# Loading residual rows earlier, two sums on another engine, and a reordered turn in a two-layer attention and MLP kernel

## The chip, the cores and the metric

The kernel runs on one core of one Trainium2 chip. The metric is the time of one execution on the device, in microseconds (us), as a median over several runs.

Five engines matter. TensorE (PE in the profile) multiplies matrices, VectorE (DVE) and ScalarE (ACT) work on elements, GpSimd (POOL) issues part of the transfers, and the DMA engines move data. Each engine executes its own queue; semaphores make one wait for another.

## The reference, cut to what matters

Two layers, each an attention part A and a token-mixing MLP part B, with residual additions, on x of 2048 rows by 1024 columns in bf16:

```python
# A: h = layernorm(x); q, k, v = h @ wqkv, 32 heads of 32
W, dil = 8, 2                      # each row attends to 8 rows: itself and every second one before it
idx = pos[:, None] - (jnp.arange(W) * dil)[None, :]
logits = einsum("bhsd,bhswd->bhsw", q, k[idx]) * scale      # masked where idx < 0
o = einsum("bhsw,bhswd->bhsd", softmax(logits), v[idx])
x = x + o @ wo
# B: h = layernorm(x); mixes over the 2048 rows, F = 3584
x = x + (gelu(h.T @ w1 + b1) @ w2 + b2).T
# ... and both once more
```

Rows of even and of odd position never attend to each other. The kernel calls them the two classes (c = 0 and 1), 1024 rows each, eight tiles of 128 rows.

## The kernel before

For each class the attention runs over two blocks of heads of four head groups each; with two classes there are four blocks, n = 0 to 3. For a block VectorE multiplies queries by shifted keys (`T`, 2.28 us each), TensorE sums these products per head (`sc`), a softmax follows on VectorE and ScalarE, and the probabilities `Pb` go out to memory (`pd`) and come back spread over the partitions (`pb`). VectorE multiplies them by the values (`pr`) and adds the eight products of each row; the sums (`oT`) feed the output projection. All work is written as generators that are woven together, and the order within each engine's queue is then settled by a scheduler when the kernel is built.

```python
def softmax_back(self, n):
    nc.vector.tensor_tensor(out=m4[:], in0=L[:, 0:4, :], in1=L[:, 4:8, :], op=ALU.add)
    ...                                            # two more sums, a reciprocal
    nc.vector.tensor_tensor(out=Pb[:], in0=L[:], in1=..., op=ALU.mult)
    nc.gpsimd.dma_start(out=dst, in_=Pb[:]...)     # pd <- Pb
    self.spread(n)                                 # two loads pb <- pd, 1 MB each

def pv(self, n, dq):                               # block n, head group dq
    for hf in range(2):                            # two halves of the rows
        pr = tpl.tile([P, 4, W, TB], BF16, name="pr", tag="T")
        ...                                        # two products pr <- pb, v
        if (n, dq) in self.pe_pv:                  # sum on TensorE: eight identity matmuls into PSUM
            for s in range(W):
                nc.tensor.matmul(acc[:]..., lhsT=ident[:], rhs=pr[:, :, s, :], start=(s == 0), stop=(s == W - 1))
            nc.scalar.copy(out=oT[:, hf * HT:(hf + 1) * HT], in_=acc[:])
        else:                                      # sum on VectorE in three steps
            for wd in (4, 2):
                nc.vector.tensor_tensor(out=pr[:, :, 0:wd, :], ..., op=ALU.add)
            nc.vector.tensor_tensor(out=dst, in0=pr[:, :, 0, :], in1=pr[:, :, 1, :], op=ALU.add)
```

The output projection of one class takes eight row tiles; for class 0 the residual rows `xr` are added by an identity matmul on TensorE. The loop loads each tile's rows at its start, from GpSimd:

```python
for i in range(NT):
    xr = x2("xr")                                  # x2: a pool with four slots
    nc.gpsimd.dma_start(out=xr[:], in_=res[i])
    ...
    for n in range(NDC):
        for kt in range(KD):
            nc.tensor.matmul(ps[:], lhsT=at_.oT[c][kt][:, i * P:(i + 1) * P], rhs=wo_t[n][kt // 4][:, kt % 4, :], ...)
        nc.tensor.matmul(ps[:], lhsT=ident[:], rhs=xr[:, xs_], start=False, stop=True)
```

Two more places are touched. At the start, eight transposed tiles `hT` are copied out of PSUM, half of them by VectorE and half by ScalarE. At the turn from layer 0 to layer 1, the last tiles of class 1 pass a layernorm (`hb`) on ScalarE, a transpose on TensorE and a copy to `hT`, and the first keys and queries of class 1 follow.

## Time and profile before

| | before |
|---|---|
| median of the first 3 runs | 1375.02 us (1372.79 to 1375.53) |
| span of the profiled run | 1371.8 us |
| TensorE busy | 1290.6 us, 94% |
| TensorE idle | 81.2 us |
| VectorE busy | 664.7 us, 48% |
| ScalarE busy | 494.0 us, 36% |

The profile also cuts the span into 40 slices of 34.3 us. A digit is the busy share of a slice in tenths, and PEclk is the clock that TensorE was granted, in tenths. TensorE's and its clock's rows for the kernel before:

```profile
PE   5899996999999999999997989979999999999997
...
PEclk9999998999999999999999999999999999999999
```

Between the opening and the last slice there are few digits under 9: the seventh (206 to 240 us, layer 0's first output projection; its clock falls too), and the 22nd, 24th and 27th, of which the 27th (892 to 926 us) is the same place in layer 1.

### The profile page before, as it was taken

What the parts mean: (1) busy time and instruction counts of PE and PEld (TensorE: products, weight loads), DVE (VectorE), ACT (ScalarE), POOL (GpSimd) and SP (SyncE); (2) the same over time, 40 slices, a digit from 0 to 9 for tenths busy, and PEclk for the clock granted to TensorE, in tenths of its full rate; (3) what the DMA queues carried; (4) which work ended last, traced back from release to release, by engine and by line L of the source; (5) the groups of instructions that cost most, each with busy time, mean ns of one, the idle gap of its engine ahead of it and who ended that gap; (6) DMA issues with size and microseconds to landing.
All of it is one profiled execution on the core that took longest, in us unless ns stands there. A gap on an engine that the chain in (4) does not pass through costs nothing.

```text
span 1371.8 us, 15564 instructions
## 1 busy us (share of the span) xinstructions
PE 1290.6 (94%) x6306; PEld 584.9 (43%) x6432; DVE 664.7 (48%) x782; ACT 494.0 (36%) x860; POOL 95.9 (7%) x231
## 2 busy tenths in 40 slices
PE   5899996999999999999997989979999999999997
PEld 3444332444444444444443434434444444444443
DVE  5366999879602332225774117976783034111111
ACT  6945443853222430123534455548322234000000
POOL 3000000100100000000001000001010000000000
PEclk9999998999999999999999999999999999999999
DMA  9134344382623235552758631335635232334341
GB/s 246 46 92 124 97 111 122 104 211 72 191 62 92 73 118 170 176 169 65 190 150 201 185 123 62 102 82 162 153 108 153 62 92 70 113 100 139 99 122 49
DMA packets 213753, 166.71 MB, mean 122 GB/s; under 512 B 6833, under 2 KB 201393, under 8 KB 211633
## 3 DMA queue, kind: packets, MB, share of 16 engines
q1 hardware_dynamic: 198656, 110.11, 28.5%
q0 software_dynamic: 14448, 54.55, 13.8%
q8 instruction: 50, 0.82, 0.3%
q10 hardware_dynamic: 576, 1.05, 0.2%
q14 instruction: 23, 0.18, 0.0%
HBM read 146.81 MB, written 18.87 MB: 121 GB/s over the span
## 4 chain that ended last, share of the span: by engine, by line
PE 67%; issue 7%; ACT 6%; DVE 3%; DMA 3%; POOL 0%; POOLq 0%; ACTq 0%
PE ps L580 27%; PE ps L602 23%; PE ps L375 10%; PE ps L547 5%; DMA w<-in_B_w_dram 1%; DMA xr<-xb 1%; PE sc L402 1%; ACT xn L551 1%; DMA xr<-in_A_x_dram 1%; DVE xo L607 1%; ACT h L229 1%; ACT h L218 1%; PE tp L234 1%; DVE pr L455 1%; DVE pr L467 1%
## 5 line engine op out<-in xcount | busy, mean ns | idle before, releaser
L602 PE MATMUL ps<-g,w 128*128 128x512 bf16 x1750 | 389.8, 380 | 8.8 <-DMA w<-in_B_w_dram 6.3
L580 PE MATMUL ps<-h,w 128*128 128x512 bf16 x1754 | 386.1, 379 | 4.1 <-ACT h L229 2.2
L375 PE MATMUL ps<-hT,wq 128*128 128x512 bf16 x1128 | 261.4, 385 | 10.3 <-ACT hT L302 4.2
L602 PEld LDWEIGHTS <-w 128*128 128x128 bf16 x1792 | 174.5, 98 | 218.9 <-DMA w<-in_B_w_dram 7.3
L580 PEld LDWEIGHTS <-w 128*128 128x128 bf16 x1792 | 175.3, 98 | 214.3 <-issue 3.3
L397 DVE TENSOR_TENSOR T<-q,k 128x4096 bf16<-128x4096 bf16 x64 | 144.0, 2288 | 107.5 <-ACT q L377 62.4
L607 DVE SCALAR_TENSOR_TENSOR xo<-ps,b_sb,xs 128x512 bf16<-128x512 f32 x64 | 48.0, 750 | 301.8 <-PE ps L602 285.7
L375 PEld LDWEIGHTS <-wq 128*128 128x128 bf16 x1152 | 114.2, 101 | 149.8 <-issue 26.0
L591 DVE TENSOR_TENSOR tmp<-ps,g 128x512 f32<-128x512 f32 x80 | 55.3, 692 | 202.3 <-PE ps L580 198.2
L467 DVE TENSOR_TENSOR pr<-pr 128x2048 bf16<-128x2048 bf16 (+1 forms) x128 | 120.5, 949 | 0.3
L547 PE MATMUL ps<-wo,oT 128*128 128x512 bf16 x376 | 95.7, 386 | 8.5 <-DVE oT L469 8.0
L455 DVE TENSOR_TENSOR pr<-pb,g 128x2048 bf16<-128x2048 bf16 x64 | 77.3, 1220 | 31.9 <-DMA pb<-pd 19.3
L592 ACT ACTIVATE g<-tmp,b_sb 128x512 bf16<-128x512 f32 x80 | 57.7, 721 | 82.1 <-DVE tmp L591 82.1
L375 PE MATMUL ps<-hT,wv 128*128 128x512 bf16 x372 | 86.1, 380 | 0.9 <-issue 0.4
L380 ACT CAST k<-ps 128x1024 bf16<-128x1024 f32 x64 | 64.6, 1014 | 46.0 <-PE ps L375 32.3
L455 DVE TENSOR_TENSOR pr<-pb,v 128x2048 bf16<-128x2048 bf16 x64 | 76.4, 1217 | 5.5 <-DMA pb<-pd 5.5
L586 ACT CAST g<-ps 128x512 bf16<-128x512 f32 x80 | 46.2, 586 | 76.0 <-PE ps L580 73.5
L547 PEld LDWEIGHTS <-oT 128*128 128x128 bf16 x384 | 37.4, 99 | 66.1 <-issue 15.1
L191 ACT ACTIVATE ln<-mv,eps 128x1 f32<-128x1 f32 x34 | 10.0, 293 | 141.8 <-DVE mv L200 137.5
L375 PEld LDWEIGHTS <-wv 128*128 128x128 bf16 x384 | 42.3, 114 | 41.8 <-issue 5.5
L377 ACT CAST q<-ps 128x512 bf16<-128x512 f32 x64 | 37.4, 588 | 53.1 <-PE ps L375 51.9
L588 ACT ACTIVATE g<-ps,b_sb 128x512 bf16<-128x512 f32 x32 | 22.0, 687 | 83.2 <-PE ps L580 83.2
(97 smaller groups left out, 703.9 us busy)
## 6 DMA issues: line engine op xcount, KB each, us to landing
w<-in_B_w_dram SPq DMA_DIRECT2D x96, 448.0 KB, 4.7
w<-in_B_w_dram SPq DMA_DIRECT2D x56, 512.0 KB, 4.8
wq<-in_A_wqkv_dram SPq DMA_DIRECT2D x40, 512.0 KB, 3.8
pb<-pd POOLq DMA_DIRECT2D x16, 1024.0 KB, 11.4
wo<-in_A_wo_dram SPq DMA_DIRECT2D x16, 512.0 KB, 3.8
xa<-xn POOLq DMA_DIRECT2D x32, 256.0 KB, 2.4
xs<-xa POOLq DMA_DIRECT2D x32, 256.0 KB, 4.3
wv<-in_A_wqkv_dram SPq DMA_DIRECT2D x12, 512.0 KB, 9.4
```

Source lines behind the costliest of these rows:

```text
L375: nc.tensor.matmul(ps[:], lhsT=cols, rhs=self.hT[c][hf][:, kt, :], start=(kt == 0), stop=(kt == KD - 1))
L380: nc.scalar.copy(out=window(buf, 0, PADK + hf * HT, [(KW + 1, 2), (1, HT)]), in_=ps[:].unsqueeze(1).to_broadcast([P, 2, HT]))
L397: nc.vector.tensor_tensor(out=T[:], in0=q[:].unsqueeze(1).to_broadcast([P, 4, SC]), in1=window(k, par, 2, [(2, 4), (1, SC)]), op=ALU.mult)
L455: nc.vector.tensor_tensor(out=pr[:, :, u, :], in0=pb[:, :, u, :], in1=window(v, par, 2 + hf * HT, [(TB, 4), (2, 4), (1, TB)]), op=ALU.mult)
L467: nc.vector.tensor_tensor(out=pr[:, :, 0:wd, :], in0=pr[:, :, 0:wd, :], in1=pr[:, :, wd:2 * wd, :], op=ALU.add)
L547: nc.tensor.matmul(ps[:], lhsT=at_.oT[c][kt][:, i * P:(i + 1) * P], rhs=wo_t[n][kt // 4][:, kt % 4, :], start=(kt == 0), stop=(kt == KD - ...
L580: nc.tensor.matmul(ps[:], lhsT=wt[c][:, i, fl * P:(fl + 1) * P], rhs=h2[c][i // 4][:, i % 4, dc * 512:(dc + 1) * 512], start=(k == 0), sto ...
L586: nc.scalar.copy(out=gs, in_=ps[:])
L591: nc.vector.tensor_tensor(out=tmp[:], in0=ps[:], in1=gs, op=ALU.add)
L592: nc.scalar.activation(out=gs, in_=tmp[:], func=ACT.Gelu_apprx_tanh, bias=b1_sb[:, ft:ft + 1])
L602: nc.tensor.matmul(ps[:], lhsT=w2t[ft // HF][:, ft % HF, c::DIL], rhs=g[ft // GF][:, ft % GF, dc * 512:(dc + 1) * 512], start=(ft == 0), s ...
L607: nc.vector.scalar_tensor_tensor(out=xo[:, dc * 512:(dc + 1) * 512], in0=ps[:], scalar=b2_sb[:, i, c:c + 1], in1=xs[:, dc * 512:(dc + 1) * ...
```

## The change

Four things at once: the residual rows are fetched two tiles ahead; two of the sums of layer 0 (head groups 2 and 3 of the second block) move from VectorE to TensorE, so that the output projection doesn't wait for VectorE; one hT copy goes from ScalarE to VectorE; and at the turn the first keys and queries of class 1 are made per half of the rows, with the last two layernorms on VectorE.

```diff
-            copy = nc.vector.tensor_copy if i % 4 in (1, 2) else nc.scalar.copy
+            copy = nc.scalar.copy if i in (0, 3, 4) else nc.vector.tensor_copy
@@ proj_pair
+            if c and pair == 0 and 0 in parts:
+                for hf in range(2):
+                    for part in parts:
+                        for dt in range(2):
+                            yield self.proj(c, part, dt, hf)
+                return
             for part in parts:
                 for hf in range(2):
@@ out_proj
+        xrs = []
+
+        def fetch():
+            if len(xrs) < NT:
+                xrs.append(x2("xr"))
+                nc.gpsimd.dma_start(out=xrs[-1][:], in_=res[len(xrs) - 1])
+
+        fetch()
+        fetch()
         for i in range(NT):
-            xr = x2("xr")
-            nc.gpsimd.dma_start(out=xr[:], in_=res[i])
+            xr = xrs[i]
...
+            fetch()
             nc.gpsimd.dma_start(out=dst_v[i], in_=xn[:])
@@ for li in range(2)
-        at_ = Attn(li, hT, ())
+        at_ = Attn(li, hT, {(1, 2), (1, 3)} if first else ())
...
-                    yield from gemm2_tile(1, i, w2_tiles(i), xa[0], xb[1][i * P:(i + 1) * P, :], hT, on_act=True)
+                    yield from gemm2_tile(1, i, w2_tiles(i), xa[0], xb[1][i * P:(i + 1) * P, :], hT, on_act=i < NT - 2)
```

## The prediction

> **What bounds the kernel now.** I read the busy table first, then TensorE's waits, then the stretches around the longest of them instruction by instruction.
>
> ```profile
> PE 1290.6 (94%) x6306; PEld 584.9 (43%) x6432; DVE 664.7 (48%) x782; ACT 494.0 (36%) x860; POOL 95.9 (7%) x231
> ```
>
> TensorE is busy for 1290.6 of 1371.8 us. From 309 us to 652 us and from 995 us to the end it hardly waits, so nothing in those stretches can give much back. What the change can win is some part of TensorE's 81 us of idle time, and what it adds to TensorE costs its full length wherever TensorE had work. The list of TensorE's waits says where the idle time is (columns: total, times, longest):
>
> ```profile
> PE ps L550 <- DMA xr<-xb: 8.6, 2, 8.3
> PE ps L547 <- DVE oT L469: 8.0, 1, 8.0
> ...
> PE ps L550 <- DMA xr<-in_A_x_dram: 5.6, 2, 5.0
> PE tp L234 <- ACT hb L229: 5.0, 6, 2.7
> PE ps L375 <- ACT hT L302: 4.2, 2, 3.1
> ```
>
> Five single waits matter, and each has a part of the change aimed at it: 8.3 and 5.0 (residual rows), 8.0 (a PV sum on VectorE), 2.7 (the last layernorm of the second class, ScalarE) and 3.1 (an hT copy). The residual wait of layer 1, in TensorE's timeline:
>
> ```profile
> 893.11 0.62 PE L402 MATMUL sc<-T,sel 128*32 128x512 bf16 x8
> 902.05 0.58 PE L550 MATMUL ps<-xr,ident 128*128 128x512 bf16 x1 [8.33 <-DMA xr<-xb]
> 902.43 3.00 PE L547 MATMUL ps<-wo,oT 128*128 128x512 bf16 x7
> ```
>
> and GpSimd's, which issues these loads in order:
>
> ```profile
> 886.29 1.05 POOL L440 DMA_DIRECT2D pb<-pd  x2 [3.90 <-DMA pd<-Pb]
> 887.31 0.61 POOL L540 DMA_DIRECT2D xr<-xb  x1
> ```
>
> The row tile that TensorE wants at 893.7 is issued at 887.3, just behind two 1 MB loads of probabilities, and lands at 902.05, 14.7 us later; the usual time to landing of this load is 3.1 us. Layer 0 has the same picture: issued at 226.9 behind the pair at 225.3, wanted at 233.2, landed at 238.2. The first tile's rows (issued at 35.9 and 793.6) wait for nothing.
>
> The wait for a PV sum:
>
> ```profile
> 212.74 1.89 PE L375 MATMUL ps<-hT,wq 128*128 128x512 bf16 x8
> 222.65 0.61 PE L547 MATMUL ps<-wo,oT 128*128 128x512 bf16 x1 [8.02 <-DVE oT L469]
> ```
>
> VectorE is busy for 96.6 of the 98 us from 139 to 237 us; the sum TensorE waits for is the third of the four halves that the change moves (pair groups 2 and 3 of the second head block), ended at 222.6.
>
> There is a second price after a long wait: the seven L547 from 902.43 take 3.00 us, 0.43 us each, against 0.216 us in steady running (eight L547 in 1.73 us). In 902.0 to 905.5 us nine 512-column matmuls take 3.5 us instead of 1.9, with a granted clock of 0.56. By the same count I get about 1.6 us of slow matmuls after the wait at 238.2 (clock 0.50), 1.6 after 222.65 (0.51) and 1.4 after the 3.13 us wait at 33.93 (0.54 to 0.69). The waits of 2.2 and 2.7 us at 195.9 and 806.9 have no such tail.
>
> **What the Trainium skill says.** "TensorE: Matmul & The Clock Gate", Part 1 (the HAM clock gate): after about one 3.4 us window of idleness the array falls to half clock and needs about as long a busy window to recover. The trace agrees: tails of 3 to 4 us at 0.43 us a matmul after waits of 5 to 8 us, none after 2.7 us. "DMA: Bandwidth & Descriptors", SWDGE vs HWDGE vs iDMA: DMAs issued from GpSimd go through rings of which only one queue is allocated, drained packet by packet; so the rows stand behind the probabilities. The trace agrees: 14.7 us against 3.1. "VectorE: DVE Perf Modes", the perf-mode tier table: a bf16 SBUF tensor_tensor runs at 2x at most, 1224 ns for 2048 elements; the trace has 1215 ns for that form of the sums, so they can't be made cheaper on VectorE and moving them is the only saving.
>
> **The change part by part.** All counts are as of TensorE, since the path is TensorE's work plus its waits.
>
> *Rows two tiles ahead.* The number of loads stays. The tile 1 load moves to directly behind tile 0's, hence to about 36 to 50 us and 794 to 802 us, far ahead of the probabilities; what now follows the probabilities is tile 2, wanted only at about 240 and 912 us and landed at about 233 and 902. The x2 pool has four slots; tile i+2 can take a slot when tile i has used its rows, which is the depth of before, so no new wait need arise. Removed: layer 1 8.33 + 0.29 + 1.6 of slow clock = 10.2 us; layer 0 5.0 + 0.58 + 1.6 = 7.2 us. VectorE waits on these same stalls (6.33 us until 906.2 and 5.4 us until 242.4, both for score matmuls stuck behind TensorE's), so it moves forward along with TensorE and the output projection of class 1, at 336 and 1008 us, doesn't turn into a wait. That matters: there VectorE finishes its last sum at 337.5 and 1009.0, level with TensorE. I take 90%: 15.7 us.
>
> *Two PV sums on TensorE.* Two head groups, two halves each: four times (1.215 + 0.684 + 0.42) = 2.32 us leave VectorE, 9.3 us. In come 4 x 8 identity matmuls at 0.216 us = 6.9 us on TensorE and four ScalarE copies of 0.58 us on an engine that is a third busy there. For the third half, VectorE is now two removed halves earlier (4.6 us): its product ends near 212.8, and sum and copy end near 216. TensorE reaches the output projection at 214.6 plus three sums (5.2 us), 219.8, so the 8.0 us wait and its 1.6 us tail go. Net 9.6 - 6.9 = 2.7 us; I take 2.5.
>
> *The eighth hT copy to VectorE.* Now on ScalarE, at 32.9 behind junk and v work; VectorE does its copy of the seventh tile at 30.35 in 0.64 us and could do this one by 31.7. TensorE's 3.13 us wait becomes about 0.9, without the tail: 3.6 us on the spot. But ScalarE is busy nearly without a gap from 30 to 70 us, and TensorE waits for its hT copies at 48 to 54 us (3.0 us in all); ScalarE gains only the 1.0 us copy and an earlier k. I let 1.5 us through.
>
> *Keys by half, and the last two layernorms on VectorE.* At the turn of layer 1 TensorE runs two projection units (16 matmuls, 3.6 us), waits 2.72 for the layernorm, transposes, then waits 1.10 for the hT copy:
>
> ```profile
> 800.53 3.62 PE L375 MATMUL ps<-hT,wq 128*128 128x512 bf16 x16
> 806.86 0.62 PE L234 MATMUL tp<-ident,hb 128*128 128x128 bf16 x8 [2.72 <-ACT hb L229]
> 808.58 10.52 PE L375 MATMUL ps<-hT,wq 128*128 128x512 bf16 x47 [1.10 <-ACT hT L239]
> ```
>
> The new order has four units that need only the first half, 7 us. On VectorE the layernorm is two statistics of 0.69, one of 0.21, ln and exp of 0.5 and the 0.55 scale, some 3 us with handovers, where ScalarE takes about 6.5; in class 0, where it is already on VectorE, TensorE's waits for it are 0.3 us at most. VectorE is idle there. Gain 2.72 + 1.10 + 0.42 (tile 6) = 4.2, of which I take 3.8. In layer 0 the order changes nothing: T needs the seventh unit either way.
>
> Sum: 15.7 + 2.5 + 1.5 + 3.8 = 23.5 us, to 1351.5.
>
> **Rivals.**
> 1. *Another engine takes the place of the wait.* In the first output projection ScalarE needs about 5.2 us a tile and TensorE 3.9; VectorE is full up to 237 us. For it: several end times lie level. Against it: each of these engines is itself held up by the waits that go. If half of the rows' gain and the sums' gain were taken back: about 1361.
> 2. *The rows are late anyway.* If the new load takes its place behind the probabilities all the same, or its slot comes free late because layernorm tiles hold the pool, only the other parts act: about 1367. Against it: the first tile's load was issued 190 us and 90 us early in the same pool.
> 3. *The sums are a loss.* If TensorE had other work to put in the 8 us gap, or the sums stall in order behind VectorE's products, they cost their 6.9 us: about 1358.
> 4. *More than the sum.* VectorE ends layer 0's class 0 some 9 us earlier, which could also remove the small score waits (0.2 to 2.2 us) and let everything through in full: about 1346.
>
> **Range and chances.** The measured waits and tails give an upper sum near 27 to 30 us (the 2% line is 27.5 us, 1347.5); instruction order is set anew by the scheduler at build time, which costs a few us more often than it gives. I predict 1352.0, 1345 to 1362. Faster by over 2% needs nearly every term in full: 0.22. Slower by 2% would need a new stall larger than all seen here: 0.01.
>
> **What would show it.** In the changed profile: no wait of L550 on xr above 1 us and no slow matmuls behind it (layer 1 should lose about 10 us between 880 and 950 us of the old clock); no wait of L547 for a PV sum at the start of the output projection, with 32 new identity matmuls and 12 fewer tensor_tensor on VectorE; the wait at the turn of layer 1 under 1 us; the wait at 33.9 us near 1 us with those for hT just after it grown. It is wrong if the row loads still follow the probabilities, if TensorE's idle time near 340 or 1010 us grows above 2 us, or if its total idle time falls by less than 20 us.

## More of the kernel before

A word on line numbers: the change adds lines, so one instruction has different numbers in different kernels. Before and after, in this order: the product T is L397 and L403, its score matmul L402 and L408, the probabilities L422 and L428, the products with the values L455 and L461, the output projection L547 and L561, its row addition L550 and L564. Experiments shift them by one at times.

## The result, and the profile after

| | median | runs | ratio to before |
|---|---|---|---|
| before | 1375.28 us (1372.79 to 1381.48) | 4 | |
| after | 1361.76 us (1356.69 to 1361.86) | 4 | 0.9886 [0.9846, 0.9926] |
| after, run again with the experiments | 1357.72 us (1356.27 to 1363.10) | 6 | 0.9870 [0.9849, 0.9891] |

A ratio is the mean time of one kernel's runs over the mean of the other's runs in the same rounds, so it isn't quite the ratio of the medians beside it. The change is faster by 1.1 to 1.3%. The time of the first comparison lies at the upper edge of the predicted range. The profiled span fell from 1371.8 to 1360.1 us.

The busy table of the kernel after:

```profile
PE 1296.8 (95%) x6338; PEld 587.5 (43%) x6464; DVE 661.2 (49%) x779; ACT 486.2 (36%) x843; POOL 96.3 (7%) x231
```

TensorE has 32 matmuls more and is busy for 6.2 us longer, its idle time is 1360.1 - 1296.8 = 63.3 us. It fell by 17.9 us, where the prediction asked for at least 20. The same two rows of slices, after:

```profile
PE   5899999799999999999998899999999999999996
...
PEclk9999999899999999999999899999999999999999
```

The digits below 9 at the 24th and 27th slice are gone. The one of the seventh slice has moved to the eighth (238 to 272 us), and the low clock with it. The second low clock, in the 23rd slice, stands behind a wait of 4.01 us for MLP weights at 750.35 us, which no part of the change aims at. So the two layers must be looked at apart. I do that with marks in TensorE's timeline, in us:

| mark | before | after |
|---|---|---|
| layer 0, first MLP matmul | 274.41 | 275.82 |
| layer 1, first projection | 598.83 | 599.68 |
| layer 1, first output projection | 884.64 | 881.83 |
| layer 1, first MLP matmul | 945.87 | 932.75 |
| last matmul's end | 1362.0 | 1350.3 |

From layer 1's first projection to the end it was 763.2 us and is 750.6 now: 12.6 us gained, more than the whole span shows. Layer 0 gained nothing. Layer 1's place of the old 8.33 us wait, TensorE's timeline after (start, duration, engine, line, operation):

```profile
892.59 0.38 PE L564 MATMUL ps<-xr,ident 128*128 128x512 bf16 x1
892.90 0.61 PE L408 MATMUL sc<-T,sel 128*32 128x512 bf16 x8
893.45 13.99 PE L375 MATMUL ps<-hT,wq 128*128 128x512 bf16 x62
```

There is no wait for rows here or anywhere else in the trace, and 62 matmuls follow in 13.99 us, 0.226 us each, so no slow tail either. From the output projection's start to the MLP's start it was 61.2 us and is 50.9: 10.3 us, against 10.2 predicted. The turn:

```profile
803.80 0.62 PE L234 MATMUL tp<-ident,hb 128*128 128x128 bf16 x8
804.25 12.03 PE L375 MATMUL ps<-hT,wq 128*128 128x512 bf16 x54
```

Neither the transpose nor the projection behind it waits any more.

Layer 0 is another matter. TensorE's waits for T in its list of waits, before and then after (total, times, longest):

```profile
PE sc L402 <- DVE T L397: 3.8, 5, 2.2
```

```profile
PE sc L408 <- DVE T L403: 11.3, 7, 5.0
```

The waits for rows and for the PV sum are gone, but waits for T, 3.8 us in all before, are 11.3 us now. The two longest in TensorE's timeline:

```profile
261.50 1.04 PE L408 MATMUL sc<-T,sel 128*32 128x512 bf16 x8 [5.02 <-DVE T L403]
264.88 1.05 PE L408 MATMUL sc<-T,sel 128*32 128x512 bf16 x8 [2.34 <-DVE T L403]
265.86 2.99 PE L561 MATMUL ps<-wo,oT 128*128 128x512 bf16 x8
```

The eight matmuls behind them take 2.99 us, 1.1 us more than the usual 1.89: a slow tail as well. Why does VectorE deliver T so late? VectorE's timeline before, around the probabilities of the third block (n = 2):

```profile
217.37 0.95 DVE L421 RECIPROCAL m<-m 128x128 f32<-128x128 f32 x1
218.23 1.16 DVE L467 TENSOR_TENSOR pr<-pr 128x2048 bf16<-128x2048 bf16 x1
219.31 1.21 DVE L422 TENSOR_TENSOR Pb<-L,m 128x1024 bf16<-128x1024 f32 x1
```

And after:

```profile
216.45 2.28 DVE L403 TENSOR_TENSOR T<-q,k 128x4096 bf16<-128x4096 bf16 x1
218.65 0.41 DVE L425 TENSOR_TENSOR m<-m 128x256 f32<-128x256 f32 x1
218.99 2.28 DVE L403 TENSOR_TENSOR T<-q,k 128x4096 bf16<-128x4096 bf16 x1
221.19 0.28 DVE L426 TENSOR_TENSOR m<-m 128x128 f32<-128x128 f32 x1
221.39 2.28 DVE L403 TENSOR_TENSOR T<-q,k 128x4096 bf16<-128x4096 bf16 x1
223.59 0.94 DVE L427 RECIPROCAL m<-m 128x128 f32<-128x128 f32 x1
224.45 2.22 DVE L403 TENSOR_TENSOR T<-q,k 128x4096 bf16<-128x4096 bf16 x1
226.60 1.21 DVE L428 TENSOR_TENSOR Pb<-L,m 128x1024 bf16<-128x1024 f32 x1
240.75 2.36 DVE L461 TENSOR_TENSOR pr<-pb,g 128x2048 bf16<-128x2048 bf16 x2 [12.94 <-DMA pb<-pd]
```

The steps of the softmax depend on one another, and the scheduler puts other work between them. Before, that was pieces of the sums and a product with the values, of 0.4 to 1.2 us. Now the sums are on TensorE, the product comes earlier, and in their place stand four products T of 2.28 us, each ahead of a step that the probabilities need. Pb starts at 226.60 instead of 219.31. GpSimd's timeline shows what follows, after:

```profile
228.10 0.64 POOL L431 DMA_DIRECT2D pd<-Pb  x1
233.39 1.05 POOL L446 DMA_DIRECT2D pb<-pd  x2 [4.65 <-DMA pd<-Pb]
```

Before, these two stood at 220.81 and 225.30. VectorE, which had work until 237 us in the kernel before, now runs out of it at 227.8 and waits 12.94 us for pb. The products with the values, and behind them the next T, come later, and TensorE waits for that T. The Trainium skill, "TensorE: Matmul & The Clock Gate", section "Architectural detail: the array is 16× 32×32, not 1× 128×128", calls VectorE's queue strictly first in, first out. The trace fits: ScalarE had cast the queries of the next T by 241.56 us, but that T stood behind the products and sums and ran at 259.16.

### The profile page after: what moved, and what is told of

It reads as the page before. It is cut to its first block, busy times and chain, and to the rows that moved or that the text cites.

```text
span 1360.1 us, 15621 instructions
## 1 busy us (share of the span) xinstructions
PE 1296.8 (95%) x6338; PEld 587.5 (43%) x6464; DVE 661.2 (49%) x779; ACT 486.2 (36%) x843; POOL 96.3 (7%) x231
## 4 chain that ended last, share of the span: by engine, by line
PE 74%; DVE 9%; ACT 6%; DMA 6%; issue 4%; POOL 1%; POOLq 0%; DVEq 0%; ACTq 0%
PE ps L595 27%; PE ps L617 23%; PE ps L375 15%; PE ps L561 5%; DVE pr L461 3%; DMA w<-in_B_w_dram 2%; DVE pr L473 2%; PE sc L408 2%; DMA pb<-pd 2%; DVE T L403 1%; DVE xo L622 1%; PE tp L234 1%; DMA b_bf<-in_B_b_dram 1%; DMA pd<-Pb 1%; DVE bn L198 1%
## 5 line engine op out<-in xcount | busy, mean ns | idle before, releaser
L473 DVE TENSOR_TENSOR pr<-pr 128x2048 bf16<-128x2048 bf16 x120 | 112.5, 944 | 0.3
```

The source lines that it names most:

```text
L473: nc.vector.tensor_tensor(out=pr[:, :, 0:wd, :], in0=pr[:, :, 0:wd, :], in1=pr[:, :, wd:2 * wd, :], op=ALU.add)
```

## The experiments

The theory after this reading: in layer 0 the four T products ahead of the probabilities take back what the other parts give. Rivals: the sums just cost TensorE their 6.9 us wherever VectorE's products stand; or the rows are worth less than I thought in layer 0; or what is missing is in the opening and the turn.

All twelve runs gave correct results. All were timed in five rounds. The median of the kernel before was 1377.46 us in the first call's rounds, 1377.02 in the second's and 1374.46 in the third's.

| run | what it is | median us | ratio to before |
|---|---|---|---|
| no_sums | after, all PV sums on VectorE | 1354.09 | 0.9833 [0.9819, 0.9848] |
| sums_pb_first | after, four T queued behind Pb | 1352.88 | 0.9835 [0.9810, 0.9860] |
| rows_only | before, rows part alone | 1358.83 | 0.9874 [0.9858, 0.9890] |
| sums_only | before, sums part alone | 1374.33 | 0.9984 [0.9972, 0.9997] |
| after_again | after | 1357.72 | 0.9870 [0.9849, 0.9891] |
| sums_one | after, only one head group on TensorE | 1355.55 | 0.9852 [0.9833, 0.9870] |
| turn_only | before, keys and layernorms parts alone | 1370.21 | 0.9950 [0.9934, 0.9966] |
| copy_only | before, hT copy part alone | 1375.97 | 0.9996 [0.9977, 1.0014] |
| one_half_late | sums_one, half a group behind Pb | 1352.30 | 0.9833 [0.9812, 0.9853] |
| one_both_late | sums_one, a whole group behind Pb | 1356.61 | 0.9862 [0.9839, 0.9885] |
| keys_only | before, keys part alone | 1371.73 | 0.9976 [0.9959, 0.9993] |
| norms_only | before, layernorms part alone | 1370.86 | 0.9965 [0.9946, 0.9983] |

For layer 0 I also add up TensorE's waits from 188 to 284 us in each trace, together with the sums it was given (eight matmuls of 0.216 us a half: 6.9 us for two head groups, 3.5 for one). Slow tails are not in it:

| trace | waits: T | PV sum or product | rows | other | sums on TensorE | total |
|---|---|---|---|---|---|---|
| before | 2.4 | 8.0 | 5.6 | 1.1 | 0 | 17.1 |
| after | 9.6 | 1.3 | 0 | 0.6 | 6.9 | 18.4 |
| rows_only | 2.7 | 8.0 | 0 | 1.9 | 0 | 12.7 |
| sums_only | 7.9 | 1.3 | 0.4 | 0.6 | 6.9 | 17.1 |
| no_sums | 3.1 | 7.9 | 0 | 1.9 | 0 | 12.9 |
| sums_pb_first | 2.9 | 1.3 | 0 | 1.9 | 6.9 | 13.0 |
| sums_one | 10.1 | 0.4 | 0 | 0.4 | 3.5 | 14.4 |
| one_half_late | 5.0 | 0.2 | 0 | 0.4 | 3.5 | 9.1 |
| one_both_late | 2.8 | 4.9 | 0 | 1.8 | 3.5 | 13.0 |

### no_sums: the change without its sums

```diff
-        at_ = Attn(li, hT, {(1, 2), (1, 3)} if first else ())
+        at_ = Attn(li, hT, ())
```

> The changed kernel with all PV sums left on VectorE. Theory A (the sums leave short VectorE work that used to fill the gaps between the dependent softmax steps; four 2.28 us products took its place, so the probabilities of layer 0's third block left 7 us later and that ate the gain of the rows there): about 1355 us, 5 to 8 us under the changed kernel, probabilities stored near 220 us again, the 8 us wait for a PV sum back, no wait of score matmuls for T above 3 us near 260. Theory B (in layer 0 the round trip of the probabilities bounds this place anyway, the rows were never worth anything there): 1360 to 1363, with the same wait for T near 260.

The median was 1354.09 us, a ratio of 0.9833 [0.9819, 0.9848]. That interval does not touch the one of the change itself in its larger repeat, 0.9870 [0.9849, 0.9891]. Pb starts at 220.35 us again and no wait for T is left near 260 us, as theory A had it. The 8 us wait for the PV sum is back in full (7.93 us at 223.69), and still the kernel is faster by 0.0037 x 1377 = 5 us. So the two sums on TensorE cost some 5 us in this kernel, although they remove the wait at which they aim.

### sums_pb_first: the sums stay, the order goes back

The four T products of the fourth block are queued behind the probabilities of the third on VectorE. Nothing else changes, no instruction is added or taken away.

```diff
+                with tc.issue_after(self.pb_ins) if self.li == 0 and n == 3 and dq < 2 else nullcontext():
                     nc.vector.tensor_tensor(out=T[:], in0=q[:]..., in1=window(k, par, 2, [(2, 4), (1, SC)]), op=ALU.mult)
...
-            nc.vector.tensor_tensor(out=Pb[:], in0=L[:], ..., op=ALU.mult)
+            self.pb_ins = nc.vector.tensor_tensor(out=Pb[:], in0=L[:], ..., op=ALU.mult).ins
```

> The changed kernel, both PV sums on TensorE, but the four products T of block 4 in layer 0 are queued on VectorE behind the probabilities Pb of block 3. Theory A: Pb ends near 219.5 instead of 227.8 us, the waits of score matmuls for T near 260 (5.0 and 2.3 us and about 1 us of slow clock) go, 1352 to 1355 us. Theory B: time within 1.5 us of the changed kernel, 1360 to 1363.

The median was 1352.88 us, 0.9835. VectorE's timeline in this run:

```profile
218.85 1.22 DVE L429 TENSOR_TENSOR Pb<-L,m 128x1024 bf16<-128x1024 f32 x1
220.00 8.89 DVE L404 TENSOR_TENSOR T<-q,k 128x4096 bf16<-128x4096 bf16 x4
232.03 2.36 DVE L462 TENSOR_TENSOR pr<-pb,g 128x2048 bf16<-128x2048 bf16 x2 [3.14 <-DMA pb<-pd]
```

Pb starts 7.75 us earlier than in the change, VectorE's wait for pb is 3.14 us (and 3.50 a little later) instead of 12.94, and TensorE has no wait for T left between 200 and 270 us. Layer 0's first MLP matmul comes at 267.07 us instead of 275.82. With the same instructions and only their order on VectorE changed, the lost time is back: the order is the cause, shown. (The interval overlaps a little with that of the change in its repeat; compared group by group, as under after_again, the runs are 5 to 6 us apart.) But the ratio equals that of no_sums. With a good order the sums are worth nothing: the table has 13.0 us of waits and sums against 12.9 without them.

### rows_only

```diff
+        fetch()
+        fetch()
         for i in range(NT):
-            xr = x2("xr")
-            nc.gpsimd.dma_start(out=xr[:], in_=res[i])
+            xr = xrs[i]
...
+            fetch()
             nc.gpsimd.dma_start(out=dst_v[i], in_=xn[:])
```

> The kernel before with only the rows fetched two tiles ahead. Theory A: layer 1 gains 9.9 us and layer 0 5 to 7, so 1357 to 1360 us. Theory B: only layer 1 gains, 1364 to 1366.

The median was 1358.83 us, 0.9874: 0.0126 x 1377 = 17.3 us. In the traces the first MLP matmul of layer 0 comes at 266.46 instead of 274.41 us (8.0 us), and layer 1's output projection takes 50.9 instead of 61.2 us (10.3 us). Together that is 18.3 us, a little more than the timed gain, which is as much as the entire change brings. So the rows are worth what was predicted, and the rival that they are late anyway is out.

### sums_only

```diff
-        at_ = Attn(li, hT, ())
+        at_ = Attn(li, hT, {(1, 2), (1, 3)} if first else ())
```

> The kernel before with only the two PV sums on TensorE. Theory A: the probabilities leave 7 us later here too, so the sums cost rather than gain: 1375 to 1381 us. The prediction's working (sums worth 2.5 us): 1372 to 1373.

The median was 1374.33 us, 0.9984 [0.9972, 0.9997]: 2.2 us gained, close to the 2.5 of the prediction. Theory A, which wanted a loss, missed in the number. But the trace shows that the number is right by accident. The bad order is here too, VectorE's timeline:

```profile
226.07 1.21 DVE L422 TENSOR_TENSOR Pb<-L,m 128x1024 bf16<-128x1024 f32 x1
239.42 2.36 DVE L455 TENSOR_TENSOR pr<-pb,g 128x2048 bf16<-128x2048 bf16 x2 [12.13 <-DMA pb<-pd]
```

With the probabilities late, their loads are issued at 232.32 us, and the row load that stood behind them in the kernel before is now issued at 222.34, ahead of them. The 5.6 us wait for rows in layer 0 falls to 0.4 with no help from the rows part, and 5.5 us more waiting for T stand in its place. So the delay of the probabilities pays for itself here by removing the row wait. In the full change the row wait is removed anyway, and only the cost is left. This explains why the two parts don't add: the product of the four ratios alone (0.9874 x 0.9950 x 0.9996 x 0.9984) is 0.9805, the change measured 0.9870, some 9 us worse; without the sums the product is 0.9821, and no_sums measured 0.9833.

### after_again

No edit: the changed kernel a second time, beside the others.

> The changed kernel once more, as it was, beside the others of this call: 1357 to 1362 us, ratio to before 0.987 to 0.990. If it lies at 1355 or below, what the earlier runs said of the sums was chance.

It gave 1357.72 us, with runs in two groups: 1356.27 to 1357.87 us four times, 1362.7 and 1363.1 us. The first comparison had three runs at 1361.7 to 1361.9 and one at 1356.69. The two profiled executions, of the two comparisons, both belong to the slower group and show the same order on VectorE (Pb at 226.60 and 228.64 us, waits of 12.94 and 13.11 us for pb). The order is fixed at build, so the step of some 5 us between the groups comes from elsewhere. It goes with the granted clock: 0.992 or 0.993 in the five faster runs of the changed kernel, 0.988 to 0.990 in the five slower ones. As an estimate from these, 0.4% of 1360 us is 5.4 us, the size of the step. I have no trace of a run of the lower group, so what lowers the clock stays open. sums_pb_first falls into two groups as well: 1349.15 to 1352.88 us at 0.992 to 0.995, and 1357.08 and 1357.25 us at 0.990. The mean of each lies 5 to 6 us under the changed kernel's group, so what the forced order gained is not a matter of which group was met.

### sums_one

```diff
-        at_ = Attn(li, hT, {(1, 2), (1, 3)} if first else ())
+        at_ = Attn(li, hT, {(1, 2)} if first else ())
```

> The changed kernel with only the first of the two PV sums on TensorE (group 2 of the second head block), the second left on VectorE as short work between the softmax steps. Theory A (order on VectorE): Pb ends at 218 to 220 us without any forced order, the 8 us wait for a PV sum is at most 3, half the TensorE cost (3.5 us): 1350 to 1353 us. Rival (moving sums costs TensorE what it saves, so half of it changes nothing): like no_sums and sums_pb_first, 1353 to 1355. If a sum on TensorE as such did the damage: 1357 to 1359, half way.

The median was 1355.55 us, 0.9852, a miss for my theory, which wanted 1350 to 1353. The order is good (Pb at 218.77 us) and half of the sums' cost is saved. TensorE's timeline shows where it failed:

```profile
215.62 0.39 PE L561 MATMUL ps<-wo,oT 128*128 128x512 bf16 x1 [0.41 <-DVE oT L475]
...
256.57 1.04 PE L408 MATMUL sc<-T,sel 128*32 128x512 bf16 x8 [6.75 <-DVE T L403]
```

The wait for the PV sum is down to 0.41 us, but TensorE runs dry later, waiting 6.75 us for T. The chain from the probabilities over their way through memory, the products and the next T sets the end of this stretch. TensorE reaches that end earlier now and only waits longer there. Moving a sum off VectorE helps only if the probabilities themselves come earlier. That is what the last two order experiments test.

### one_half_late and one_both_late

On top of sums_one, the work of head group 3 is queued behind Pb on VectorE: of its second half (4.7 us), or of both halves.

```diff
             for hf in range(2):
+                with tc.issue_after(self.pb_ins) if self.li == 0 and (n, dq, hf) == (1, 3, 1) else nullcontext():
-                pb = self.pbs[(n, hf)]
+                    pb = self.pbs[(n, hf)]
...                                                # products and sum of this half, inside the with
```

In one_both_late the condition is `(n, dq) == (1, 3)`.

> All of the change, with the sums of one head group alone on TensorE, and the second half of the other group (two products, one sum in three steps, 4.7 us on VectorE) queued behind the probabilities of the third block. Theory A (layer 0's first output projection is bound by the chain probabilities, their way through memory, products, score operand): the probabilities start near 215 us instead of 218.8, VectorE's first wait for them shrinks by some 3 us, TensorE's 6.75 us wait for T at 256.6 falls to about 3, time about 1352, ratio 0.982 to 0.984. Theory B (the end of that stretch is set by VectorE's total work or by the order in which TensorE gets its work, not by the probabilities' date): the wait comes back elsewhere, for the sum of the second half or for T, and the ratio stays at 0.985 to 0.987.

> As one_half_late, but both halves of that head group behind the probabilities (9.3 us of VectorE's work). Theory A: the probabilities start near 212 us, some 6 us earlier than with one group alone, and the T wait at 256 us nearly goes; against that the first half of that group's sum comes some 4 us later (near 219 instead of 215.5) and TensorE waits up to 3 us for it: ratio 0.980 to 0.984. Theory B: the sum's wait of 8 us is back near 215 to 223 us, T's wait stays near 6, ratio 0.986 to 0.989.

one_half_late had 1352.30 us, 0.9833. Pb starts at 215.44 us, and TensorE's timeline has this:

```profile
214.27 0.39 PE L561 MATMUL ps<-wo,oT 128*128 128x512 bf16 x1 [0.22 <-DVE oT L475]
...
251.58 0.61 PE L408 MATMUL sc<-T,sel 128*32 128x512 bf16 x8 [1.88 <-DVE T L403]
```

Pb comes 3.3 us before sums_one's, and the wait for T falls from 6.75 to 1.88 us. That is what the theory of the chain says, in date and in wait. The ratio lies where it wanted it (0.982 to 0.984), but its interval overlaps widely with that of sums_one (0.9833 to 0.9870), so the gain in time is not shown apart from noise. one_both_late had 1356.61 us, 0.9862, at the very start of the rival's range of 0.986 to 0.989 and outside of 0.980 to 0.984. Pb is earlier still, at 212.78 us, and T's wait there is gone as the theory had it, but the sum comes later than I allowed:

```profile
221.81 0.61 PE L561 MATMUL ps<-wo,oT 128*128 128x512 bf16 x1 [4.90 <-DVE oT L475]
```

4.90 us instead of at most 3. In the ledger that makes 13.0 us against 9.1. The two needs, an early Pb and an early oT, pull VectorE's order in opposite directions, and half a group looks like the better split of those tried. This is not shown in time: the two intervals overlap by a little, and one_both_late's runs fall into two groups again, 1351.98 and 1352.31 us (the traced one is the first) against 1356.61 to 1359.23 us at a lower clock. The faster ones are level with one_half_late's.

### turn_only, keys_only, norms_only

turn_only has both parts at the turn, the other two one each.

```diff
+            if c and pair == 0 and 0 in parts:     # keys_only and turn_only
+                for hf in range(2):
+                    for part in parts:
+                        for dt in range(2):
+                            yield self.proj(c, part, dt, hf)
+                return
...
-                    yield from gemm2_tile(1, i, ..., hT, on_act=True)
+                    yield from gemm2_tile(1, i, ..., hT, on_act=i < NT - 2)     # norms_only and turn_only
```

> The kernel before with only the key order and the last two layernorms on VectorE. The prediction's working: the waits of 2.72, 1.10 and 0.42 us in layer 1 go, 3.8 us, ratio near 0.997. Rival: VectorE or the load of weights takes the place, under 1.5 us, ratio above 0.999.

> The kernel before with only the first class-1 keys and queries laid out by half. The pair of keys and layernorms gave 0.995 (6.9 us) where 3.8 was predicted. Theory A (each hides part of the same 3.8 us): the four units that need only the first half cover the 2.72 us wait for the layernorm and most of the 1.10 for the copy, 3 to 4 us alone, ratio 0.997 to 0.998, and the two parts together are worth less than their sum. Theory B (the order also helps elsewhere, in layer 0's turn): ratio 0.995 to 0.996 alone, with TensorE's stretch from 200 to 280 us shorter by 2 us or more.

> The kernel before with only the last two class-1 layernorms of layer 0 on VectorE. Theory A: the 2.72 us wait for hb goes to under 0.5 and the 1.10 for hT stays: 2.5 to 3 us, ratio 0.998. Theory B (the layernorms on ScalarE also held up its copies of projections behind them, so more than the visible wait goes): 5 us or more, ratio 0.995 to 0.9965.

The ratios were 0.9950, 0.9976 and 0.9965, that is 6.9, 3.3 and 4.8 us of the rounds' medians of before. TensorE's transpose of the last tile in keys_only and in norms_only, which waited 2.72 us before:

```profile
811.48 0.62 PE L234 MATMUL tp<-ident,hb 128*128 128x128 bf16 x8 [0.34 <-ACT hb L229]
```

```profile
804.76 0.62 PE L234 MATMUL tp<-ident,hb 128*128 128x128 bf16 x8
```

Either part alone removes nearly all of that wait, and in both the projection behind it waits no more. From layer 1's first projection to its first output projection, before needs 285.8 us, keys_only 282.8, norms_only 281.8 and turn_only 281.6. At the place itself the gain is thus 3.0, 4.0 and 4.2 us. These three can't be told apart by the stretch alone, which also holds two waits for MLP weights: in the four traces with the old turn (before, rows_only, sums_only, copy_only) it takes 285.7 to 287.8 us, in the eight with both parts 280.4 to 282.7. But the waits at the turn say it directly: each part alone removes most of the same waits, so the two parts overlap, as theory A had it. The 1.10 us wait for hT, which theory A left in norms_only, is gone there too, and its 4.8 us lie nearer to theory B. Theory B of keys_only isn't borne out: from the end of the wait for T, at 200.18 and before at 195.94 us, to layer 0's first MLP matmul it takes 78.2 us against 78.5 before.

The timed ratio of turn_only is larger, 6.9 us with an interval of 4.7 to 9.1. The trace of before is a fast one at this place: between the means of those four and eight traces lie 5.4 us. In the other three traces with the old turn the projection behind the waits of 2.72 and 1.10 us has a slow tail, 12.04 us up to the next projection instead of 10.36. The intervals of the two single parts do not exclude either theory.

### copy_only

```diff
-            copy = nc.vector.tensor_copy if i % 4 in (1, 2) else nc.scalar.copy
+            copy = nc.scalar.copy if i in (0, 3, 4) else nc.vector.tensor_copy
```

> The kernel before with only the eighth hT copy moved to VectorE. The prediction's working: 1.5 us let through, ratio 0.999. From the changed kernel's trace (2.0 us ahead at 32 us, 0.2 us at 74 us, ScalarE full from 34 to 54 us): 0 to 0.5 us, ratio 0.9995 to 1.0005, not to be told from before.

The ratio was 0.9996 [0.9977, 1.0014]: no effect that five rounds can show. The projection that waits for the copy starts at 31.96 us instead of 33.93, and its wait is 2.09 instead of 3.13 us, but its 32 matmuls take 8.77 us, as long as before (8.75). I had counted on the slow tail going with the shorter wait, and it didn't. The same holds in the full change. TensorE's clock there, in stretches of its trace (us, busy time and number of instructions of each engine, then the granted clock, DMA share, GB/s):

```profile
31.90:36.00 4.10, 4.07 (x12) 1.51 (x13) 3.89 (x9) 4.04 (x12) 0.54 (x1) 0.58 0.13 31
...
195.00:200.00 5.00, 4.16 (x17) 1.30 (x16) 4.97 (x4) 1.43 (x2) 0.00 (x0) 0.66 0.02 6
```

The clock is 0.58 behind a wait of 2.03 us, and 0.66 behind one of 2.28 us at 195.84. The kernel before had a wait of 2.21 us at the latter place with no slow tail.

## Why the prediction was right or wrong

The time fell in the range, 0.24 us from its upper end, and "within 2%" was the likeliest in the prediction. The steps behind it did not all hold, and that the number did is partly luck: the sums cost some 5 us instead of giving 2.5, and the turn, perhaps the rows too, gave more than was taken. One of the prediction's own signs of being wrong came true, TensorE's idle time fell by 17.9 us and not by at least 20.

- **Rows two tiles ahead: right, in mechanism and size.** Predicted 10.2 us for layer 1, measured 10.3 in the trace; predicted 7.2 for layer 0, measured 8.0 in rows_only. Whether the 10% that I kept back for other engines was needed can't be told: rows_only's 17.3 us have an interval of 15.1 to 19.6, which holds both 15.7 and 17.4. In layer 0 tile 2's rows are issued at 167.76 us in the change, earlier than the prediction had them; in layer 1 they follow the probabilities, as it said.
- **The two PV sums: the step that failed.** The prediction said that VectorE "is now two removed halves earlier" and gave the sums a net gain of 2.5 us. The aimed-at wait did go, from 8.02 us to a new one of 1.25 us for a product. What failed is the assumption that taking work off VectorE leaves the rest in its order. The scheduler filled the gaps between the softmax's steps with four T products, Pb started 7.3 us later, and TensorE's waits for T between 188 and 284 us grew from 2.4 to 9.6 us. Measured in place of the +2.5: about -5 us beside the other parts (after_again against no_sums), +2.2 alone, and 0 with the order mended (sums_pb_first against no_sums).
- **VectorE "moves forward along with TensorE": wrong in layer 0.** The sentence was about the rows, and in rows_only it holds: T's waits there are 2.7 us. Together with the sums it fails, and layer 0's share of the rows, 7.2 us, is not seen in the change at all.
- **Two rivals came near.** Rival 1, about 1361 us, is nearest to the first comparison: a wait takes the place of the one removed. But I looked for it in ScalarE's time per tile and in how full VectorE is, and it came from VectorE's order. Rival 3, sums at a loss, gave 1358, which is nearest to the repeat (1357.72). It has the right part at a loss, for a different reason: it charged their 6.9 us to TensorE, where the loss lay in the order. The reservation in the range, that the order is set anew at build time, was the right worry with too small a number.
- **The turn: right in place, low in size.** Both waits of 2.72 and 1.10 us are gone, and turn_only's trace shows 4.2 us there against 3.8 taken. The timing says 4.7 to 9.1 us, and the difference between the means of four and eight traces is 5.4. What the prediction missed is a slow tail: it wrote that a wait of 2.7 us has none, from the one trace that it had, and three other traces have one of 1.7 us at this place.
- **The hT copy: too high.** 1.5 us was taken; the measured ratio is 0.9996, its interval from 3.2 us gained to 1.9 lost. The wait shrank by 1 us only, not to 0.9, and the tail stayed.
- **The sum.** Predicted 23.5 us, measured 13.5 between the medians and 17.9 in the repeat's ratio (0.0130 x 1377). Without the sums, 0.0167 x 1377 = 23 us are there, against 21.0 taken for the other parts.

Three versions have lower ratios than the change: no_sums (0.9833), sums_pb_first (0.9835) and one_half_late (0.9833), the latter two with intervals that still overlap its interval by 0.0011 and 0.0004. They can't be told apart in these runs, although one_half_late has the shortest ledger in layer 0 and the shortest profiled span, 1348.0 us. The simplest of them is the change with its sums left on VectorE.

## What to carry to other kernels

Work that is moved off an engine leaves gaps in that engine's queue, and what the scheduler puts there can delay a chain of small steps on which a transfer, and later the busiest engine, depend; look in the new trace for what now stands between the dependent steps. Two parts that remove waits at the same place are not to be added up, and a part that measures as a small gain alone can do so by trading one wait for another. When a part has taken away its own wait and the time has not moved, find the next date on the path (here the start of the probabilities) and move that, with an ordering edge rather than with more engines.

## What the Trainium skill lacked or had wrong

- "TensorE: Matmul & The Clock Gate", Part 1, puts half clock after at least one idle window of about 3.4 us. Here TensorE ran at a granted clock of 0.58 behind a wait of 2.03 us and 0.66 behind one of 2.28 us, while a wait of 2.21 us at the latter place in another run had no slow tail. The waits of 2.72 and 1.10 us at the turn have no tail in the trace of before and one of 1.7 us in three others. Waits shorter than the stated window can have a slow tail, and whether they do differs from trace to trace; the prediction's "the trace agrees" rested on one trace, in which the 3.13 us wait already had a tail. The page does say that the window runs free and that the number of slow matmuls varies from run to run.
- "DMA: Bandwidth & Descriptors", SWDGE vs HWDGE vs iDMA, says that one queue serves the transfers issued from GpSimd. The landing times fit: issued behind the two 1 MB loads the rows took 14.7 us to land, and issued ahead of them no wait was left. The page has no number for such queueing.
- No page that I read warns that the build-time order of an engine's queue moves when work is taken out of it. Here this was worth 7.3 us in the start of one instruction and some 5 us of the total.
